# Copies between engines, the rank of the experts and four held-back output pairs in a fused attention and mixture-of-experts kernel

## The chip, the cores and the metric

The kernel runs on one core of one Trainium2 chip. The metric is the device time of one execution in microseconds. Before the change three timed executions took 368.27, 366.48 and 367.61 us; their median is 367.61 us. Inputs and outputs lie in the chip's HBM, and all arithmetic is on the core.

## What is computed

Two blocks follow each other. The first is a linear attention over 8 batches of 576 tokens, 8 heads of 64 values each: the state kv = kᵀv of each head is multiplied by q, normed by its root mean square and scaled by `g_norm`. The second is a mixture of 8 experts over the 4608 tokens of 512 values that come out. A token with a positive score against `w_skip` goes through the one expert that its gate picks.

```
kv  = einsum('bhsd,bhse->bhde', k, v)
o   = einsum('bhsd,bhde->bhse', q, kv)
x   = o / sqrt(mean(o*o, -1) + 1e-6) * g_norm          # as rows: N = 4608, D = 512
out = x.copy()
for the rows with x @ w_skip > 0:
    e      = argmax(x @ w_gate)                         # of 8 experts
    out[row] = x + softmax(x @ w_gate)[e] * (relu(x @ w1[e]) @ w2[e])
```

## The kernel before

All instructions stand in an order that the program itself writes out (`tc.manual_schedule()`), so each engine executes its list strictly in that order, and a waiting instruction holds up all that stands behind it on its engine or queue.

**The attention part** runs over 36 units (`units`): a unit is a half of the heads (u = 0 or 1) for four of the nine token groups of a batch; a pair of units (u = 0 and 1) makes one output tile `xb` of x, 128 x 1024 values, called pair `nq`. Every fourth batch is followed by two units for the ninth token group of the four batches. One step n of the loop over `NU + 2` steps issues, in this order: `turn(n + 1)`, which transposes q of the next unit on TensorE (line 460) and copies it out on ScalarE (L463); `root(n - 1)`, a square root on ScalarE (L529); the jobs of part "early"; `values(n)`, the products q·kv on TensorE (L498, or L508 for the ninth group) and their squares on ScalarE (L514); the jobs of part "mid"; `norm(n - 1)` on VectorE (L536, the reciprocal; L545, `xl` = the product scaled); `squares(n)`, the sums of squares on VectorE (L522); the jobs of part "pe"; then the next jobs of the gating streams. From step 30 on `squares(n)` stands ahead of `norm(n - 1)`. `values` writes one of two PSUM buffers `o_ps`, or `sum_ps` at two steps near the end. GpSimd multiplies `xl` by `g_norm` into `xb` (L615).

**The state of a batch** (`state`, `state_t`, `state_m`) is made in steps ahead of the batch's own units: matmuls k·v (L383) into `sum_ps`, a copy `both` on ScalarE (L390), two transposes (L400) and the logit columns of the state (L408, into the PSUM bank `g_ps`, copied to the `kvd` tiles by ScalarE, L412). Each head pair of `both` also goes to `kvd` in two places: `own` by GpSimd (L395) and `other`, 64 x 256 values that change their partitions, by VectorE (L394, two copies a batch).

**Gating** works in three groups of token tiles (`ends` = 12, 22, 36). For a group, `choose` finds each token's expert on VectorE (ending with `ohb`, L685), `rank` counts on TensorE into the same bank `g_ps` which place a token takes in its expert's list (L696, L699, L702), and `number` turns this into numbers (`pr`, `top`, `s_i`, `lo_i`, `hi_k`, and the one-hot rows `oha_k`, L728). After the second group, when 22 of 36 tiles are known, `rank_experts` sorts the experts by their counts; the order is read back into registers of the DMA queue SyncE (`order_i`, L814), which can then load the first expert's weights w1 (L337). `early` finds the first 192 rows of the first expert: `put` places them on TensorE (L924, 22 matmuls that read `bv`, L904), sums them on VectorE (L928), and gathers their x from the output in HBM by indirect DMAs on GpSimd (L917); TensorE turns these rows (L848, waiting for the gather) and starts the first expert's first layer (L859).

**DMA queues.** SyncE (SP) issues the loads of k, v and q (L118), most stores of x (L653; L642 for the ninth group), and the weights (L337 for w1, L347 for w2). GpSimd issues the first half of every second pair's store (L649) and all indirect DMAs. The stores of two pairs (8 and 9) are held back until step 24 (`store_from`, `starts[B - 3] + 2`). The tile `room`, 128 x 4096 values, is the place of the first expert's w2; until that load it holds small setup data in its first and third quarter. The load of w2 is issued at step 32, behind `values(32)`.

**The expert part** runs on from there over the 8 experts, each with its own w1 and w2 (2 MB each), gathers of its rows, two layers, and scattered stores. The change does not touch it.

Of the kernel before, what the change touches and what calls it, by code (L numbers as in the profile page):

```python
# [8 lines left out]
FP32 = mybir.dt.float32  # L9
BF16 = mybir.dt.bfloat16  # L10
I32 = mybir.dt.int32
# [6 lines left out]
def kernel(  # L18
# [227 lines left out]
    nc.vector.tensor_copy(out=ebase[:, :], in_=ebase_i[:, :])  # L246
    exp_f = keep.tile([P, E], FP32)
# [106 lines left out]
    kvTs, boths = {}, {}  # L354
# [5 lines left out]
    def other(b, w):  # L360

        return kvds[b % KVD][(1 - w) * 64:(2 - w) * 64, w, 1 - w, :, :]
# [12 lines left out]
    def state(b, some):  # L375

        kt, vt = kts[b], vts[b]
        for i in some:
            u, c = divmod(i, C)
            for w in range(2):  # L380
                for a in range(2):
                    r = slice(a * 64, (a + 1) * 64)
                    nc.tensor.matmul(  # L383
                        out=sum_ps[w * 64:(w + 1) * 64, a, u, :],
                        lhsT=kt[r, 2 * u + w, c, :], rhs=vt[r, 2 * u + w, c, :],
                        start=(c == 0), stop=(c == C - 1), skip_group_check=True)
        if some.stop < 2 * C:
            return
        both = att_pool.tile([P, 2, 2 * D], FP32, tag="both", name="both", bufs=1)
        nc.scalar.copy(out=both[:, :, :].rearrange("p u (a d) -> p a u d", a=2), in_=sum_ps)  # L390
        boths[b] = both
        cols = slice(G, G + 2 * D)
        for w in range(2):
            nc.vector.tensor_copy(out=other(b, w)[:, :, cols], in_=both[w * 64:(w + 1) * 64, :, :])  # L394
            nc.gpsimd.tensor_copy(out=own(b, w)[:, :, cols], in_=both[w * 64:(w + 1) * 64, :, :])  # L395

    def state_t(b):
        both = boths.pop(b)
# [223 lines left out]
    store_from = {x[0]: starts[B - 3] + 2 for x in units if x[1:3] in ((0, None), (4, 0))}  # L622
# [12 lines left out]
    def store_x(nq, b, i):  # L635
# [11 lines left out]
        first = int(i == 1 and b < B - 1)  # L647
# [119 lines left out]
    order_i = keep.tile([1, E], I32)  # L767
# [7 lines left out]
    def rank_experts():  # L775

        key = count_tokens("key", gat_pool)
        nc.vector.scalar_tensor_tensor(out=key[:, :], in0=key[:, :], scalar=float(E),
                                       in1=eorder[:, :], op0=ALU.mult, op1=ALU.add)
# [16 lines left out]
        order_f = gat_pool.tile([P, E], FP32, tag="order_f", name="order_f")  # L796
        yield
        nc.vector.tensor_reduce(out=order_f[:, :], in_=gt[:, :, :], axis=AX.X, op=ALU.add)
        yield
        nc.vector.tensor_copy(out=order_i[:, :], in_=order_f[0:1, :])  # L800
# [3 lines left out]
            in0=order_f[:, :].unsqueeze(2).to_broadcast([P, E, CK]), scalar=float(RSPACE // 128),  # L804
# [91 lines left out]
    def early():  # L896
# [24 lines left out]
        def put():  # L921
            scale(now[0])
            for t in range(NE):
# [3 lines left out]
            rows = gat_pool.tile([P, 2], FP32, tag="rows1", name="rows1")  # L927
            nc.vector.tensor_reduce(out=rows[:, :], in_=ps.rearrange("p (c i) -> p c i", i=2),  # L928
                                    axis=AX.X, op=ALU.add)
            gather(rows[:, 0:1], P, 0)  # L930

            def put_more():
# [4 lines left out]
            at(now[0], "pe", put_more)  # L937
# [26 lines left out]
    for b, n in starts.items():  # L964
        if b:
# [8 lines left out]
            at(step, "early", lambda b=b: state_t(b))  # L974
            at(step, "pe", lambda b=b: state_m(b))
# [7 lines left out]
    def gating(g):  # L983

        yield from choose(g)
        yield lambda: rank(g)
# [9 lines left out]
    streams = []  # L996
# [12 lines left out]
    for n in range(NU + 2):  # L1009
        now[0] = n  # L1010
        if 1 <= n < NU - 1:
            turn(n + 1)
# [615 lines left out]
```

## Time and profile before

| | before |
|---|---|
| timed executions | 368.27, 366.48, 367.61 us (median 367.61) |
| the profiled execution | 366.29 us |
| its span, first to last instruction | 364.4 us |
| mean granted TensorE clock | 0.994 |
| busy: TensorE, VectorE, ScalarE, GpSimd | 349.5, 249.2, 145.1, 125.7 us |
| read and written in HBM | 66.80 MB, 14.48 MB |

The profiled execution's own time is 1.9 us longer than its span: that is what lies around the first and the last instruction. The attention part ends near 118 us of the span, the expert part takes the rest. TensorE (PE) is called busy almost throughout, but its matmuls are pipelined and their ends modelled, so what counts is where the profile shows it idle and what ended that idle time. Rows of the timeline give the start, the duration, the engine, the line and the operation, a count if several are merged, and in brackets the idle time of the engine just ahead with what released it. "PEld" is TensorE's weight load, which runs beside its matmuls.

### The profile page before, as it was taken

The numbers are of one execution on the slowest core, as the hardware profiler recorded it, in microseconds if no ns is written. First come the engines' busy times: TensorE is split into PE (matmuls) and PEld (weight loads), VectorE is DVE, ScalarE is ACT, GpSimd is POOL, SyncE is SP. The second block draws the span as 40 slices with busy tenths as digits, with TensorE's granted clock in tenths as the row PEclk, the third lists the DMA queues.
The fourth block names the chain that finished last, engine by engine and source line by source line (L and its number), as shares of the span: only waits on it lengthen the run. The fifth ranks groups of instructions, "written<-read, shape, count | busy, mean of one in ns | idle before, by whom it ended". The sixth has DMA issues, their size and how long they took to land.

```text
span 364.4 us, 9568 instructions
## 1 busy us (share of the span) xinstructions
PE 349.5 (96%) x3754; PEld 305.5 (84%) x3754; DVE 249.2 (68%) x637; ACT 145.1 (40%) x418; POOL 125.7 (34%) x205
## 2 busy tenths in 40 slices
PE   8979998999899999999999999999999999999994
PEld 4769987888779669599879978989988998989983
DVE  2545677889888563876937676786776776878831
ACT  2537775676666244244104402512421530431420
POOL 8036777677776072123041102303203203002003
PEclk9989999999999999999999999999999999999999
DMA  8999999999797369873535537455563762601001
GB/s 272 387 390 377 371 392 398 394 394 384 247 335 255 104 208 379 340 262 89 209 107 205 171 124 254 121 224 176 175 230 98 250 235 53 243 1 58 3 2 54
DMA packets 32808, 81.70 MB, mean 224 GB/s; under 512 B 3242, under 2 KB 3250, under 8 KB 32756
## 3 DMA queue, kind: packets, MB, share of 16 engines
q1 hardware_dynamic: 28944, 69.48, 53.7%
q0 software_dynamic: 3792, 11.53, 9.3%
q8 instruction: 31, 0.51, 0.5%
q14 instruction: 21, 0.17, 0.1%
q10 hardware_dynamic: 20, 0.02, 0.0%
HBM read 66.80 MB, written 14.48 MB: 223 GB/s over the span
## 4 chain that ended last, share of the span: by engine, by line
PE 79%; issue 6%; DMA 5%; DVE 5%; POOL 2%; ACT 2%; SPq 0%; POOLq 0%; DVEq 0%; ACTq 0%
PE bank L1252 46%; PE bank L1184 9%; PE o_ps L498 6%; PE sum_ps L383 4%; PE bank L1172 3%; PE q_ps L460 3%; DMA v<-in_v_dram 2%; PE bank L1153 2%; DVE xl L545 1%; DMA xg<-out_dram,src 1%; PE g_ps L859 1%; DMA xg<-out_dram,asrc 1%; PE q_ps L859 1%; PE o_ps L479 1%; DVE rs L522 1%
## 5 line engine op out<-in xcount | busy, mean ns | idle before, releaser
L1262 ACT COPY p<-bank 128x128 f32<-128x128 f32 (+6 forms) x70 | 20.8, 297 | 96.1 <-PE bank L1252 94.6
L1252 PE MATMUL bank<-xt,w 128*128 128x128 f32 (+5 forms) x336 | 55.4, 288 | 0.1
L1383 POOL DMA_INDIRECT out_dram<-xg,rows x14 | 13.9, 996 | 116.2 <-DVE xg L1380 113.0
L1252 PEld LDWEIGHTS bank<-xt,w 128*128 128x128 f32 x336 | 47.0, 190 | 1.9 <-DVE bank L1256 1.4
L615 POOL TENSOR_TENSOR xb<-xl,g_b 128x512 f32<-128x512 f32 x34 | 41.3, 1216 | 18.1 <-DVE rs L536 16.1
L1256 DVE TENSOR_TENSOR bank<-bank,p 128x128 f32<-128x128 f32 (+6 forms) x70 | 23.6, 337 | 29.7 <-PE bank L1252 28.7
L498 PE MATMUL o_ps<-kvd,qT 128*128 128x146 f32 x240 | 36.0, 293 | 1.3 <-DVE xl L545 1.0
L1252 PE MATMUL bank<-xs,s 128*128 128x128 f32 (+5 forms) x224 | 36.7, 288 | 0.0
L498 PEld LDWEIGHTS o_ps<-kvd,qT 128*128 128x128 f32 x240 | 32.1, 192 | 2.1 <-DVE xl L545 1.8
L1252 PEld LDWEIGHTS bank<-xs,s 128*128 128x128 f32 x224 | 31.1, 190 | 1.0 <-ACT p L1262 0.8
L1184 PE MATMUL bank<-w,ht 128*32 128x128 f32 (+2 forms) x424 | 29.9, 313 | 0.0
L522 DVE TENSOR_REDUCE rs<-sq 128x8 f32<-128x512 f32 x36 | 24.5, 681 | 5.4 <-ACT sq L514 5.2
L545 DVE TENSOR_TENSOR xl<-o_ps,rs 128x584 f32<-128x584 f32 x32 | 24.5, 767 | 4.3 <-DVE rs L536 0.5
L1184 PEld LDWEIGHTS bank<-w,ht 128*32 128x32 f32 (+2 forms) x424 | 18.2, 119 | 10.6 <-issue 7.2
L1252 PE MATMUL bank<-t,ht 128*128 128x256 f32 x112 | 27.0, 384 | 0.0
L1252 PE MATMUL bank<-w,ht 128*128 128x256 f32 x112 | 26.5, 380 | 0.0
L383 PE MATMUL sum_ps<-v,k 64*64 64x64 f32 x1152 | 23.5, 223 | 3.0 <-issue 2.6
L1144 POOL DMA_INDIRECT xg<-out_dram,src x14 | 14.3, 1024 | 34.8 <-DMA out_dram<-xg,rows 18.0
L514 ACT ACTIVATE sq<-o_ps 128x512 f32<-128x512 f32 x34 | 20.3, 596 | 14.1 <-PE o_ps L498 13.2
L383 PEld LDWEIGHTS sum_ps<-v,k 64*64 64x64 f32 x1152 | 19.6, 134 | 7.1 <-issue 3.9
L1252 PE MATMUL bank<-t,hs 128*128 128x256 f32 x112 | 25.3, 379 | 0.0
L1252 PEld LDWEIGHTS bank<-t,ht 128*128 128x128 f32 x112 | 20.8, 190 | 3.9 <-issue 1.2
(216 smaller groups left out, 665.2 us busy)
## 6 DMA issues: line engine op xcount, KB each, us to landing
w<-in_moe_w_dram SPq DMA_DIRECT2D x16, 2048.0 KB, 9.0
k<-in_k_dram SPq DMA_DIRECT2D x32, 288.0 KB, 6.0
v<-in_v_dram SPq DMA_DIRECT2D x32, 288.0 KB, 6.3
q<-in_q_dram SPq DMA_DIRECT2D x32, 288.0 KB, 6.2
out_dram<-xb SPq DMA_DIRECT2D x29, 256.0 KB, 6.1
out_dram<-xb POOLq DMA_DIRECT2D x7, 256.0 KB, 6.4
xg<-out_dram,src POOLq DMA_INDIRECT x16, 3.6
out_dram<-xg,rows POOLq DMA_INDIRECT x16, 6.1
```

The lines of the kernel that those rows point to most:

```text
L383: nc.tensor.matmul(out=sum_ps[w * 64:(w + 1) * 64, a, u, :], lhsT=kt[r, 2 * u + w, c, :], rhs=vt[r, 2 * u + w, c, :], start=(c == 0), stop ...
L498: mm = nc.tensor.matmul(out=ps[:, w, 0:2 * PK].rearrange("p (r k) -> p r k", r=2)[:, :, cols], lhsT=qT[:, w, a, :], rhs=kvds[b % KVD][:, w ...
L514: nc.scalar.activation(out=sq[:, :, :, :], in_=heads(ps, G, G + 2 * D), func=ACT.Square)
L522: nc.vector.tensor_reduce(out=rs[:, :, :], in_=sq[:, :, :, :].rearrange("p x y (a d) -> p x (y a) d", a=2), axis=AX.X, op=ALU.add)
L545: nc.vector.tensor_tensor(out=xl[:, :, :, :].rearrange("p x y (a k) -> p x (y a) k", a=2), in0=ps[:, :, 0:2 * PK].rearrange("p x (h k) -> ...
L615: late.append((lambda eng: eng.tensor_tensor(out=xb[:, :, 4 * u * D:(4 * u + 4) * D].rearrange("p r (w x) -> p r w x", w=2), in0=xl[:, :, ...
L1144: nc.gpsimd.indirect_dma_start(out=x_of(xg, off, m), out_offset=None, in_=cut_rows(m)[:, :], in_offset=bass.IndirectOffsetOnAxis(ap=idx[:, ...
L1184: nc.tensor.matmul(out=yps[q * m:(q + 1) * m, 0:n], lhsT=ht(f)[:, off:off + m], rhs=w_sb[r][1][:, f, q * n:(q + 1) * n], start=(f == 0), s ...
L1252: nc.tensor.matmul(out=out, lhsT=lhsT(i), rhs=rhs(i), start=start and i == 0, stop=i == k - 1, skip_group_check=True)
L1256: nc.vector.tensor_tensor(out=to, in0=x, in1=y, op=ALU.add)
L1262: nc.scalar.copy(out=t, in_=x)
L1383: ins = nc.gpsimd.indirect_dma_start(out=cut_rows(m)[:, :], out_offset=bass.IndirectOffsetOnAxis(ap=rows[:, col:col + 1], axis=0), in_=x, ...
```

## The change

The change has five parts.

1. **Held-back pairs.** The x of pairs 2 to 5 (both halves of batches 1 and 2) is written into the four quarters of `room` in place of `xb` buffers, and all eight half stores of 256 KB go out on SP behind the last load of q at step 24, in place of six on SP and two on GpSimd at various steps ahead.
2. **Copies across.** For batches 5, 6 and 7 (`ACROSS` = 5) the two `other` copies go from VectorE to ScalarE: one behind `kvT`, one behind the squares of the same step.
3. **Ranks ahead.** `rank` of the first two groups goes from part "pe" to part "mid", so that TensorE does it directly behind `values`, ahead of `state_m`.
4. **Fewer sums for the order of the experts.** The counts come in one step with a constant `kbase` = `eorder` - 8 `ebase`, and the reduction writes `order_i` as integers at once; one subtraction and one cast fall away.
5. **Sums beside the placing.** `put` turns q of step 32 at once behind the 22 placing matmuls; the sum of the rows, both gathers and the small matmul `more` stand behind `squares(30)`. Two empty turns of the stream keep `put` at step 30, so that `lo_i`, `oha_k` and `bv` come a step earlier than they did relative to it.

```diff
@@ state
         for w in range(2):
-            nc.vector.tensor_copy(out=other(b, w)[:, :, cols], in_=both[w * 64:(w + 1) * 64, :, :])
+            if b < ACROSS:
+                nc.vector.tensor_copy(out=other(b, w)[:, :, cols], in_=both[w * 64:(w + 1) * 64, :, :])
             nc.gpsimd.tensor_copy(out=own(b, w)[:, :, cols], in_=both[w * 64:(w + 1) * 64, :, :])
+    def state_across(b, w):
+        if b >= ACROSS:
+            nc.scalar.copy(out=other(b, w)[:, :, G:G + 2 * D], in_=boths[b][w * 64:(w + 1) * 64, :, :])
@@ weigh
-            xbs[nq] = xb_pool.tile([P, 2, DM], FP32, tag="xb", name="xb")
+            if nq in IN_ROOM:
+                x = room[:, IN_ROOM.index(nq) * 2 * DM:(IN_ROOM.index(nq) + 1) * 2 * DM]
+                xbs[nq] = x.rearrange("p (r d) -> p r d", r=2)
+            else:
+                xbs[nq] = xb_pool.tile([P, 2, DM], FP32, tag="xb", name="xb")
...
-    store_from = {x[0]: starts[B - 3] + 2 for x in units if x[1:3] in ((0, None), (4, 0))}
+    IN_ROOM = range(2, 6)
+    store_from = {nq: starts[B - 3] + 2 for nq in (*IN_ROOM, 4 * NQ, 4 * NQ + 1)}
@@ store_x
-        first = int(i == 1 and b < B - 1)
+        first = int(i == 1 and b < B - 1 and nq not in store_from)
@@ rank_experts
-        key = count_tokens("key", gat_pool)
-        nc.vector.scalar_tensor_tensor(out=key[:, :], in0=key[:, :], scalar=float(E),
-                                       in1=eorder[:, :], op0=ALU.mult, op1=ALU.add)
+        key = gat_pool.tile([P, E], FP32, tag="key", name="key")
+        nc.vector.scalar_tensor_tensor(out=key[:, :], in0=top[:, :], scalar=float(E),
+                                       in1=kbase[:, :], op0=ALU.mult, op1=ALU.add)
...
-        nc.vector.tensor_reduce(out=order_f[:, :], in_=gt[:, :, :], axis=AX.X, op=ALU.add)
-        yield
-        nc.vector.tensor_copy(out=order_i[:, :], in_=order_f[0:1, :])
+            nc.vector.tensor_reduce(out=order_i[:, :], in_=gt[:, :, :], axis=AX.X, op=ALU.add)
@@ early: put
-            rows = gat_pool.tile([P, 2], FP32, tag="rows1", name="rows1")
-            nc.vector.tensor_reduce(out=rows[:, :], in_=ps.rearrange("p (c i) -> p c i", i=2),
-                                    axis=AX.X, op=ALU.add)
-            gather(rows[:, 0:1], P, 0)
-
-            def put_more():
+            turn(now[0] + 2)
+            turned_ahead.append(now[0] + 2)
+
+            def put_rows():
+                rows = gat_pool.tile([P, 2], FP32, tag="rows1", name="rows1")
+                nc.vector.tensor_reduce(out=rows[:, :], in_=ps.rearrange("p (c i) -> p c i", i=2),
+                                        axis=AX.X, op=ALU.add)
+                gather(rows[:, 0:1], P, 0)
...
-            at(now[0], "pe", put_more)
+            at(now[0], "squared", put_rows)
+        yield
+        yield
         yield "mid", put
@@ the states' steps
             at(step, "early", lambda b=b: state_t(b))
+            for w, part in enumerate(("early", "mid")):
+                at(step, part, lambda b=b, w=w: state_across(b, w))
@@ gating
-        yield lambda: rank(g)
+        yield "mid", lambda: rank(g)
@@ the loop over the steps
-        if 1 <= n < NU - 1:
+        if 1 <= n < NU - 1 and n + 1 not in turned_ahead:
             turn(n + 1)
...
             squares(n)
+        jobs(n, "squared")
```

Three places show how the change moves instructions. A row is a line of the program, the operation, and output<-input with the shape; "x4" merges four alike.

TensorE, step 24, before. `q_ps` is the transposed q of step 25, `o_ps` the products of step 24, `sum_ps` a part of the state of batch 7, and `g_ps` takes in turn the transposed state, its logit columns and the rank of the second group:

```order
L460 MATMUL q_ps<-ident,q 128x2x64 x4
L400 MATMUL g_ps<-ident,both 128x128 x2
L498 MATMUL o_ps<-kvd_161,qT 128x2x73 x4
L408 MATMUL g_ps<-gw_b,kvT 128x36 x2
L383 MATMUL sum_ps<-v,k 64x64 x16
L696 MATMUL g_ps<-top,ident 128x88
L699 LDWEIGHTS ut
L699 MATMUL g_ps<-ohb,ut 128x80
```

The same place in the changed kernel, where L709, L712 and L715 are the rank and L416 the logit columns; first the head of the rank, then its end:

```order
L468 MATMUL q_ps<-ident,q 128x2x64 x4
L408 MATMUL g_ps<-ident,both 128x128 x2
L506 MATMUL o_ps<-kvd_161,qT 128x2x73 x4
L709 MATMUL g_ps<-top,ident 128x88
L712 LDWEIGHTS ut
L712 MATMUL g_ps<-ohb,ut 128x80
```

```order
L715 LDWEIGHTS ones
L715 MATMUL g_ps<-ohb,ones 128x8
L416 MATMUL g_ps<-gw_b,kvT 128x36 x2
L386 MATMUL sum_ps<-v,k 64x64 x16
L468 MATMUL q_ps<-ident,q 128x2x64 x4
```

The rank now stands ahead of the logit columns, and so also ahead of ScalarE's copies that read them. The first group's rank, at step 16, moves in the same way.

VectorE, from the end of step 27 to step 29, before. `rs` is the sum of squares and its reciprocal, `xl` the normed product, `kvd<-both` the copies across of batch 7, and the rest the gating of the second group:

```order
L394 COPY kvd_167<-both 64x2x128 x2
L721 TENSOR_SCALAR lo_i<-s_i 128x10
L723 TENSOR_SCALAR hi_k<-s_i 128x10
L728 TENSOR_TENSOR oha_k<-row_i,lo_i 128x256 x2
L536 RECIPROCAL rs<-rs 128x8
L545 TENSOR_TENSOR xl<-o_ps,rs 128x584
L522 TENSOR_REDUCE rs<-sq 128x8
L728 TENSOR_TENSOR oha_k<-row_i,lo_i 128x256 x3
L899 TENSOR_TENSOR ohc_1975<-hi_k,colid_i 128x44
```

And in the changed kernel:

```order
L736 TENSOR_SCALAR hi_k<-s_i 128x10
L741 TENSOR_TENSOR oha_k<-row_i,lo_i 128x256 x3
L544 RECIPROCAL rs<-rs 128x8
L553 TENSOR_TENSOR xl<-o_ps,rs 128x584
L530 TENSOR_REDUCE rs<-sq 128x8
L741 TENSOR_TENSOR oha_k<-row_i,lo_i 128x256 x2
L910 TENSOR_TENSOR ohc_1970<-hi_k,colid_i 128x44
L915 TENSOR_TENSOR bv_1972<-ohc_1970,row_k 128x88
```

The two copies are gone, `lo_i` stands a step earlier, and `bv`, which the placing reads, moved up by one reciprocal, `xl` and `rs`.

VectorE behind that, before: the placed rows' sum and the first gather's indices stand ahead of the `rs` of step 30, the second gather's behind the norm.

```order
L904 TENSOR_TENSOR bv_2002<-ohc_1975,row_k 128x88
L928 TENSOR_REDUCE rows_2044<-g_ps 128x2
L913 TENSOR_SCALAR row_2047<-rows_2044,q_f_237 128x1
L915 SCALAR_TENSOR_TENSOR src_2046<-row_2047 128x1
L522 TENSOR_REDUCE rs<-sq 128x8
L536 RECIPROCAL rs<-rs 128x8
L545 TENSOR_TENSOR xl<-o_ps,rs 128x584
```

And in the changed kernel:

```order
L530 TENSOR_REDUCE rs<-sq 128x8 x2
L943 TENSOR_REDUCE rows_2048<-g_ps 128x2
L924 TENSOR_SCALAR row_2051<-rows_2048,q_f_239 128x1
L926 SCALAR_TENSOR_TENSOR src_2050<-row_2051 128x1
L924 TENSOR_SCALAR row_2057<-g_ps,q_f_250 128x1
L926 SCALAR_TENSOR_TENSOR src_2056<-row_2057 128x1
```

The sum of the rows and the first gather's indices moved behind the `rs` of step 30, and the second gather's came up to them.

More of the change, by code (lines that the diff above doesn't have):

```diff
@@ L766 @@
     colid_i = keep.tile([P, NCOL], I32)
-    order_i = keep.tile([1, E], I32)
+    order_i = keep.tile([P, E], I32)
     is_at = keep.tile([P, E, E], FP32)
@@ L994, in gating @@
             yield from early()
-    streams = []
+    streams, turned_ahead = [], []
     now = [0]
```

12 lines of the change are left out of this document (8 added, 4 removed).

## The prediction

> **What bounds the kernel now.** I looked first at the page's chain of work that ended last (PE 79% of it), then at the table of busy time by stretches, to see where TensorE is not full, and then at the timeline there. TensorE is full but for its first 30 us and a few places between 60 and 105 us, all in the part that the change touches.
>
> ```profile
> core 0: us, PE busy (x) PEld busy (x) DVE busy (x) ACT busy (x) POOL busy (x), PEclk, DMA share, GB/s
> 60.00:65.00 5.00, 4.04 (x126) 3.50 (x115) 3.13 (x10) 2.69 (x9) 2.64 (x7) 1.00 1.05 396
> 80.00:85.00 5.00, 4.34 (x103) 3.86 (x104) 4.63 (x12) 3.61 (x11) 3.96 (x7) 1.00 1.03 373
> 90.00:95.00 5.00, 5.00 (x76) 4.53 (x74) 4.57 (x14) 3.56 (x11) 3.90 (x9) 1.00 0.54 169
> 95.00:100.00 5.00, 3.33 (x34) 2.98 (x33) 4.43 (x12) 3.00 (x10) 3.95 (x7) 1.00 0.98 352
> ```
>
> TensorE lacks 0.96 us in the first of these stretches, 0.66 in the second and 1.67 in the last; in the third it lacks nothing. The DMA engines are saturated up to 85 us, but TensorE does not wait for them there.
>
> The chain of waits in order of time shows what bounds the last stretch: VectorE, up to a gather that TensorE then waits for.
>
> ```profile
> 93.04 0.29 DVE kvd L394
> ...
> 93.76 0.27 DVE lo_i L721
> 94.10 1.02 DVE oha_k L728 x2
> 95.37 0.77 DVE xl L545
> 96.72 1.09 DVE oha_k L728 x3
> ...
> 98.95 0.59 DVE rs L522
> 99.54 0.17 DVE bv L904
> ...
> 100.48 0.17 DVE rows L928
> ...
> 101.37 5.18 DMA xg<-out_dram,src
> 106.69 0.63 PE q_ps L848 x4
> 108.43 0.89 PE g_ps L859 x8
> ```
>
> From L848 on, TensorE has its work in a row up to the expert part, whose loads follow TensorE's own progress. So whatever L848 gains or loses goes to the end. The question is only how much earlier L848 starts.
>
> **The ranks.** The timeline at the first group's rank:
>
> ```profile
> 60.23 0.27 DVE L685 TENSOR_TENSOR ohb<-eorder,fi 128x96 bf16<-128x96 f32 x1
> 60.46 0.64 PE L408 MATMUL g_ps<-gw_b,kvT 128*128 128x36 f32 x4
> 62.05 0.47 PE L696 MATMUL g_ps<-top,ident 128*128 128x104 f32 x2 [0.96 <-ACT kvd L412]
> ```
>
> The rank stands behind the logit columns and waits until ScalarE has read them out of the same bank. In the new order it follows `values`, and what it needs, `ohb`, is ready at 60.50, when `values` ends (L408 starts at 60.46). Nothing reads the bank then but the copy `kvT`, which L408 needs too. The wait of 0.96 us goes. The logit columns come later by the rank's length, under 1 us, and ScalarE's four copies with them; they are for units a step away. Next is the transposed q of unit 18, then `qT`, the root and `xl`, which move up by almost as much (ScalarE ends its copies some 0.65 us later, just as q is there). I take **-0.9**, bounded by 0 and -1.07 (the weight load's idle time).
>
> The second group's rank, at step 24:
>
> ```profile
> 81.80 1.16 PE L498 MATMUL o_ps<-kvd,qT 128*128 128x146 f32 x8
> 82.01 0.73 DVE L394 COPY kvd<-both 64x256 f32<-64x256 f32 x2
> 83.13 0.49 DVE L685 TENSOR_TENSOR ohb<-eorder,fi 128x80 bf16<-128x80 f32 x1
> 84.40 0.46 PE L696 MATMUL g_ps<-top,ident 128*128 128x88 f32 x2 [0.45 <-ACT kvd L412]
> ```
>
> The idle 0.45 us goes in the same way if `ohb` is there when `values` ends, at 82.96. Before, it ends at 83.62. But the two copies ahead of it (0.73 and the gap) leave VectorE, so it ends at 82.86. The parts hang together: without the copies' move the rank would wait 0.66 us for `ohb`. I take **-0.45**; between 0 (`ohb` late again) and -0.66 (all that the stretch lacks).
>
> **The transfers held back.** Eight half stores, 2 MB, leave the queue ahead of the loads of q and k, v. TensorE has no wait for them now, so this is worth nothing by itself, but it carries the gain above: the q of unit 18 is issued here,
>
> ```profile
> 53.84 3.43 SPq L118 DMA_DIRECT2D q<-in_q_dram  x4
> DMA to landing us min/median/max: 3.2/6.2/7.5
> ```
>
> so its first two parts land at about 60 to 61.5, and TensorE now wants them at 61.9 instead of 62.8. Two stores of 256 KB less ahead at 390 GB/s are 1.3 us. Without this cover up to half of the -0.9 would be in doubt. At the other end, SP now has this in front of the first expert's weights:
>
> ```profile
> 78.02 6.06 SPq L118 DMA_DIRECT2D q<-in_q_dram  x8
> 85.77 2.85 SPq L653 DMA_DIRECT2D out_dram<-xb  x3
> 92.71 0.42 SPq L337 DMA_DIRECT2D w<-in_moe_w_dram  x1
> ```
>
> The loads of q for batch 6 come some 5 us earlier, those of batch 7 can't (their buffer is free only when step 24 has turned q, L460 ahead of 81.8), then come eight stores, the five old ones, and the experts' order. The bytes up to w1 are the same as before, so I leave w1 at about 92.7. Its cover: stores issued behind it
>
> ```profile
> L653 SPq DMA_DIRECT2D out_dram<-xb x2: 553/568/582, 93.8 to 94.5; - x2
> DMA to landing us min/median/max: 9.4/9.4/9.4
> ```
>
> landed by 103.2 to 103.9, while L859, its first use, comes at 108.4. Some 4.5 to 5 us are left. I take **0**, and price the loss of this cover below.
>
> **The chain to the gather.** Up to the `rs` of step 29, VectorE loses the copies (93.04 to 93.76, 0.72 us) and `lo_i` (0.34 with its gap, moved to where TensorE has more work than VectorE); one `oha_k` (0.36, a third of 1.09) moves a step up, and `bv` takes its place behind `ohc`. At the `xl` of 95.37 that is 0.72 + 0.34 - 0.36 = 0.70 us, and at the `rs` of 98.95 it is 0.70 + 0.36 - 0.21 = 0.85. Since ScalarE's root must fit in between, I use 0.73. Then the new order takes it back: before, from the end of `rs` (99.54) to `rows` (100.48) it is 0.94 us by `bv` and the 22 matmuls. Now it is the root, the squares, and the `rs` of step 30:
>
> ```profile
> 99.57 0.30 ACT L529 ACTIVATE rs<-rs,eps_t 128x8 f32<-128x8 f32 x1 [0.95 <-DVE rs L522]
> 99.78 0.58 ACT L514 ACTIVATE sq<-sum_ps 128x512 f32<-128x512 f32 x1
> 101.00 0.68 DVE L522 TENSOR_REDUCE rs<-sq 128x8 f32<-128x512 f32 x1
> ```
>
> 99.54 to 100.36 are 0.82, 0.68 for the sum and two gaps of 0.03 make 1.56: 0.62 more. The gather comes 0.73 - 0.62 = **0.1** earlier. Bounds: +0.6 (no VectorE time arrives) and -0.85 (the squares are done sooner). The small matmul `more` now makes TensorE wait for `rows`, with the products of step 31 behind it; but the products of step 32 waited for `xl` of step 29 anyway, so I cost it at nothing; uncovered it is about 1 us.
>
> The gather took 5.18 us. Other gathers of the kernel:
>
> ```profile
> L1144 POOL DMA_INDIRECT xg<-out_dram,src x14: 953/978/1464, 129.7 to 288.8; - x14
> DMA to landing us min/median/max: 2.9/3.6/7.1
> ```
>
> Since it now starts 1.4 us nearer to w1, it can as well take longer; between 3.6 and 7.1, and I keep 5.2 as the row that is the same place: **0**, from -1.6 to +1.9. [...]
>
> **ScalarE's copies.** A copy of that size on ScalarE:
>
> ```profile
> L482 ACT COPY q<-o_ps x15: 353/356/373, 16.5 to 103.5; 64x256 f32<-64x256 f32 x15
> ```
>
> Six of them are 2.1 us, two to a step; the first fits into ScalarE's idle time ahead of the squares (it waits for TensorE there), the second delays the four small copies by 0.36. I take **0**, up to +0.35 in each of the last two such steps. [...]
>
> The two instructions saved for the experts' order (some 0.35 us) and the setup of `kbase` lie where TensorE is full: 0.
>
> **Sum.** -0.9 - 0.45 - 0.1 = **-1.45 us**. From the profiled execution's 366.3 (its span of 364.4 and 1.9 around it) that is 364.8. That execution is the fastest of the four shown, 1.3 under the median of 367.6; against their mean, 367.2, it makes 365.7, and I say **365.8**.
>
> **The rivals.**
>
> *The gather eats the gain.* VectorE gets to the rows no earlier, or the gather takes 5.8 to 6.2 because w1 and the eight stores are still moving. For it: L848 waited for the gather before already, and everything ahead of it then only makes this wait longer. Against it: the gather starts earlier by all that TensorE gains. The kernel gains 0 to 0.9: 366.3 to 367.2.
>
> *More than the sum.* The DMA engines are emptier at 100 us, since w1 lands ahead of the gather, and it takes 3.6 to 4.5: 0.7 to 1.6 more, a gain of 2.1 to 3.1, 364.1 to 365.1. For it: the loads of q are no longer behind 2 MB of stores. Against it: these stores are now nearer to the gather.
>
> *Slower: w1 comes late.* SP stands at batch 7's q until TensorE has turned step 24's q, with nothing in front; the DMA engines run empty, and then 2 MB at 390 GB/s are 5.4 us more between q and w1. If 3 us of emptiness come on top, w1 is 8.4 us later. From 5 us on each one counts in full: L859 starts 3.4 us later, and the kernel takes 369.7 on the profile's scale. For it: a queue in order, and the reading of the experts' order (88.6 to 92.7) hidden by nothing. Against it: the same bytes went in front of w1 before, and an emptied queue lets SP issue faster.
>
> **How the numbers follow.** The forecast has 0.45, the gather 0.18, more than the sum 0.25, slower 0.12. The range reaches from the second rival's gain to the first steps of the third: 363.9 to 368.4. A measurement of this kernel tells about 0.5%, 1.8 us, from no change. The second rival and a small part of the forecast are faster by more than that, 0.32; the slower one, 0.12; the rest, 0.56, is within.
>
> **What would show it.** In the profile after, no idle time ahead of either rank; no L394 after 70 us, and `xl` of step 27 some 0.7 us nearer to the `rs` ahead; the gather starting about 100.0 and L848 at 105.3. The forecast is wrong if TensorE waits for a load of q or for `ohb`, if w1 is issued after 97, or if the gather takes other than 4.6 to 5.8.

## The result and the profile after

The changed kernel took 371.88 us (median of six runs, 370.96 to 374.46), the kernel before 367.17 us (six runs, 366.10 to 368.27). The ratio is **1.0141**, with a 95% interval of 1.0115 to 1.0167: slower by some 5 us, outside the range that was predicted. The profiled execution took 374.46 us with a span of 372.7; it is the slowest of the six. Below, a time is the median of all executions of a kernel; a ratio is taken to executions of the kernel before beside them, and leaves out single executions that took over 1.5% more than the fastest of their kernel.

Where the change acts as forecast, the profile after shows it. TensorE does both ranks without idle time ahead of them, no copy across is left on VectorE after 70 us, and the wait ahead of the products of step 29 fell from 1.02 us to 0.38. The timeline of TensorE after, the two ranks and that step:

```profile
60.07 0.47 PE L709 MATMUL g_ps<-top,ident 128*128 128x104 f32 x2
...
64.49 0.57 PE L386 MATMUL sum_ps<-v,k 64*64 64x64 f32 x21 [1.75 <-issue]
...
84.05 0.35 PE L709 MATMUL g_ps<-top,ident 128*128 128x88 f32 x2
...
96.73 1.26 PE L506 MATMUL o_ps<-kvd,qT 128*128 128x146 f32 x8 [0.38 <-DVE xl L553]
```

The row of step 29 in the timeline of the kernel before:

```profile
96.19 1.26 PE L498 MATMUL o_ps<-kvd,qT 128*128 128x146 f32 x8 [1.02 <-DVE xl L545]
```

But behind the first rank, at 64.49, stands a wait of 1.75 us for "issue" (time in which the engine waited for nothing that the profile shows), which the profile of the kernel before does not have there. It comes back below.

The large loss is further on. SP's timeline after, from the loads of q for batches 6 and 7 to the first expert's weights:

```profile
73.97 10.38 SPq L118 DMA_DIRECT2D q<-in_q_dram  x8
84.39 7.82 SPq L666 DMA_DIRECT2D out_dram<-w  x8
92.31 2.35 SPq L655 DMA_DIRECT2D out_dram<-xb  x2
94.75 3.06 SPq L666 DMA_DIRECT2D out_dram<-xb  x3
102.06 0.42 SPq L340 DMA_DIRECT2D w<-in_moe_w_dram  x1
```

The eight loads of q, the first ones issued early and the last ones held until their buffer is free, keep SP for 10.38 us where it was 6.06 before. Only then come the eight held stores (`w` is the name of the room's tile), and w1 goes out at 102.06 in place of 92.71. The table by stretches shows what the DMA engines (the last two columns, share and GB/s) did meanwhile, and the clock ahead of them:

```profile
core 0: us, PE busy (x) PEld busy (x) DVE busy (x) ACT busy (x) POOL busy (x), PEclk, DMA share, GB/s
80.00:82.00 2.00, 2.00 (x52) 1.78 (x50) 1.32 (x7) 1.43 (x4) 0.64 (x3) 1.00 0.10 38
82.00:84.00 2.00, 1.79 (x14) 1.55 (x15) 1.85 (x6) 1.95 (x6) 1.71 (x3) 1.00 0.21 33
100.00:102.00 2.00, 1.08 (x24) 0.85 (x22) 1.11 (x4) 1.72 (x5) 1.32 (x2) 1.00 0.16 53
112.00:120.00 8.00, 7.99 (x59) 7.40 (x58) 4.51 (x17) 3.22 (x12) 1.88 (x4) 0.50 1.03 390
```

From 80 to 84 the engines are nearly empty (share 0.10 and 0.21): SP stands at a load that can't start (its longest wait for TensorE's `q_ps`, L468, is 5.6 us), and 2 MB that could go stand behind it. Before, the stretch from 80 to 85 moved 373 GB/s. TensorE's timeline then shows what waits:

```profile
109.65 0.63 PE L859 MATMUL q_ps<-ident,xg 128*128 128x128 f32 x4 [2.42 <-DMA xg<-out_dram,src]
...
111.56 0.66 PE L859 MATMUL q_ps<-ident,xg 128*128 128x128 f32 x2 [0.61 <-DMA xg<-out_dram,src]
112.23 2.07 PE L870 MATMUL g_ps<-xt_first,w 128*128 128x128 f32 x8
...
115.42 4.63 PE L870 MATMUL g_ps<-xt_first,w 128*128 128x64 f32 x16
```

The same two rows of the first layer (L859 then) in the timeline of the kernel before:

```profile
108.27 1.06 PE L859 MATMUL g_ps<-xt_first,w 128*128 128x128 f32 x8
...
109.92 2.46 PE L859 MATMUL g_ps<-xt_first,w 128*128 128x64 f32 x16
```

The gather was issued at 102.54, with w1 half a microsecond ahead of it, and its rows landed 7.0 us later. The weights held the first layer up for less, as the row of its weight load in the kernel after shows:

```profile
112.23 1.78 PEld L870 LDWEIGHTS g_ps<-xt_first,w 128*128 128x128 f32 x8 [0.41 <-DMA w<-in_moe_w_dram]
```

Then the same products took almost twice as long, 4.63 against 2.46 us: the granted clock is 0.50 from 111.2 to 121.4.

Counted up between the two profiled executions: the products of step 33 start at 105.97 against 105.23 (+0.7), the first layer at 112.23 against 108.27 (+4.0), and the last matmul at 366.65 against 358.66 (+8.0). So 3.2 us arise where TensorE waits for the gather (3.0 us) and its weight load for w1 (0.4), and the other 4 us behind that, for the most part at half clock. In the six runs the mean clock lay between 0.983 and 0.992 (mean 0.9865); in 27 runs of the kernel before, taken later beside the first experiments, its mean is 0.9948. By this, 0.0083 of some 370 us, an estimate of 3.1 us of the loss is clock.

### The profile page after: what moved, and what is told of

It is laid out like the page before. It is cut to its first block, busy times and chain, and to the rows that moved or that the text cites. A ratio compares the mean times of both kernels' runs of the same rounds, so it can differ in the third digit from the quotient of the medians.

```text
span 372.7 us, 9558 instructions
## 1 busy us (share of the span) xinstructions
PE 354.1 (95%) x3754; PEld 308.8 (83%) x3754; DVE 246.6 (66%) x630; ACT 147.9 (40%) x424; POOL 125.8 (34%) x203
## 4 chain that ended last, share of the span: by engine, by line
PE 80%; issue 7%; DMA 5%; DVE 3%; POOL 2%; ACT 2%; SPq 0%; POOLq 0%; DVEq 0%; ACTq 0%
PE bank L1271 45%; PE bank L1203 9%; PE o_ps L506 6%; PE sum_ps L386 5%; PE bank L1191 4%; PE q_ps L468 3%; DMA v<-in_v_dram 3%; PE bank L1172 2%; DMA xg<-out_dram,src 2%; PE g_ps L870 2%; DVE xl L553 1%; PE q_ps L870 1%; PE g_ps L416 1%; PE o_ps L487 1%; PE g_ps L408 1%
## 5 line engine op out<-in xcount | busy, mean ns | idle before, releaser
L1275 DVE TENSOR_TENSOR bank<-bank,p 128x128 f32<-128x128 f32 (+6 forms) x70 | 23.6, 337 | 29.7 <-PE bank L1271 28.9
L627 POOL TENSOR_TENSOR xb<-xl,g_b 128x512 f32<-128x512 f32 x26 | 31.8, 1221 | 18.6 <-DVE rs L544 12.9
L386 PE MATMUL sum_ps<-v,k 64*64 64x64 f32 x1152 | 25.0, 223 | 5.9 <-issue 4.6
L386 PEld LDWEIGHTS sum_ps<-v,k 64*64 64x64 f32 x1152 | 20.5, 134 | 10.6 <-issue 7.4
L1163 POOL DMA_INDIRECT xg<-out_dram,src x14 | 15.1, 1080 | 34.5 <-DMA out_dram<-xg,rows 11.6
L522 ACT ACTIVATE sq<-o_ps 128x512 f32<-128x512 f32 x34 | 20.3, 596 | 13.9 <-PE o_ps L506 10.2
```

What stands on the lines that cost most here:

```text
L386: nc.tensor.matmul(out=sum_ps[w * 64:(w + 1) * 64, a, u, :], lhsT=kt[r, 2 * u + w, c, :], rhs=vt[r, 2 * u + w, c, :], start=(c == 0), stop ...
L522: nc.scalar.activation(out=sq[:, :, :, :], in_=heads(ps, G, G + 2 * D), func=ACT.Square)
L627: late.append((lambda eng: eng.tensor_tensor(out=xb[:, :, 4 * u * D:(4 * u + 4) * D].rearrange("p r (w x) -> p r w x", w=2), in0=xl[:, :, ...
L1163: nc.gpsimd.indirect_dma_start(out=x_of(xg, off, m), out_offset=None, in_=cut_rows(m)[:, :], in_offset=bass.IndirectOffsetOnAxis(ap=idx[:, ...
L1275: nc.vector.tensor_tensor(out=to, in0=x, in1=y, op=ALU.add)
```

## The experiments

Theory 1: all of the loss comes from part 1, the held-back stores. The rivals put it on the rows' sum behind the squares (A) or on the copies and ranks (B).

**Part 1 taken back.**

```diff
-    IN_ROOM = range(2, 6)
+    IN_ROOM = range(0)
```

> The changed kernel with part 1 alone taken back: no pair in the w2 room, all stores at the steps of before. Theory 1 (the eight stores behind the last q load push w1 back, and that costs the whole loss): w1 is issued near 92.5 us again in place of 102.06, the gather lands in about 5.2 us in place of 7.2 to 7.5, no half clock after 110 us, and the time is 365.0 to 366.7, below the kernel before by what the prediction summed (about 1.4). Rival A (the loss comes from the rows' sum behind the squares, which starts the gather later): w1 is early, yet the gather still starts near 102.5, and the time stays above 369. Rival B (the copies on ScalarE or the ranks ahead slow the steps from 40 to 80 us): TensorE's idle time there stays as in the changed kernel, and the time is 368 to 370.

Measured: 367.86 us (12 runs), ratio 0.9995 (0.9975 to 1.0016). The loss is gone, and so are the late w1 and the wait for the gather, as SP's and TensorE's timelines show:

```profile
94.44 0.42 SPq L340 DMA_DIRECT2D w<-in_moe_w_dram  x1
```

```profile
65.36 0.57 PE L386 MATMUL sum_ps<-v,k 64*64 64x64 f32 x21 [2.00 <-issue]
...
108.98 0.60 PE L859 MATMUL q_ps<-ident,xg 128*128 128x128 f32 x4
```

Rivals A and B fall. But the time is not below the kernel before either, where theory 1 had 365.0 to 366.7: what parts 2 to 5 were to bring isn't seen.

**Part 1 alone on the kernel before** (its lines of `weigh`, `store_from` and `first`, nothing else).

> The kernel before with part 1 alone: four pairs in the room, eight stores behind the last q load. Theory 1: w1 is issued at 101 to 103 us, the first layer of the first expert waits for it or for the gather beside it, and the time is 370.5 to 373. Rival A or B (the loss is in the other parts): 367 to 368, as before.

Measured: 372.61 us, ratio 1.0126 (1.0091 to 1.0160). w1 went out at 101.74, and of TensorE's waits one line carries it:

```profile
PE q_ps L853 <- DMA xg<-out_dram,src: 3.0, 1, 3.0
```

(in total, times, longest). Taking part 1 away and putting it in alone give the same answer: theory 1 holds.

**The held stores between the two loads of q.**

```diff
-    store_from = {nq: starts[B - 3] + 2 for nq in (*IN_ROOM, 4 * NQ, 4 * NQ + 1)}
+    store_from = {**{nq: starts[B - 3] + 1 for nq in IN_ROOM},
+                  **{nq: starts[B - 3] + 2 for nq in (4 * NQ, 4 * NQ + 1)}}
```

> The changed kernel with the eight held stores one step earlier, so that they stand on SP between the q loads of batch 6 and batch 7, in the time in which SP waits for the buffer of batch 7's q. Theory 1 (what costs is that the DMA engines run empty while SP waits, and 2 MB come after): the stores fill that gap, w1 is issued at 93 to 97 us and the time is 365 to 367.5. Rival C (holding the stores costs by itself, by the bytes in front of w1 wherever they stand): w1 stays later than 99, and the time is 369 to 372. A late q of batch 7 would show as idle time of TensorE ahead of L468 at step 26 to 28.

Measured: 370.33 us, ratio 1.0046 (1.0016 to 1.0076). SP's timeline:

```profile
74.60 3.27 SPq L118 DMA_DIRECT2D q<-in_q_dram  x4
77.92 7.14 SPq L666 DMA_DIRECT2D out_dram<-w  x8
85.16 3.86 SPq L118 DMA_DIRECT2D q<-in_q_dram  x4
...
96.96 0.42 SPq L340 DMA_DIRECT2D w<-in_moe_w_dram  x1
```

The stores now fill the gap (DMA share 0.97 and 0.99 from 80 to 84 us, where it was 0.10 and 0.21). From the start of step 24's products to the issue of w1 it is 11.4 us here, 10.9 before, 10.3 without held stores, but 19.0 in the changed kernel and 18.7 with part 1 alone. So the place is what made w1 late, not the bytes. The time is another matter: theory 1 had 365 to 367.5, and 370.33 lies in rival C's range. The clock is lower again, 0.9887 in the mean of 12 runs against 0.9948, and 0.0061 of 370 us is 2.3 us, an estimate as large as the loss that is left (1.7 us by the ratio). The one profile has its half clock in two stretches, and neither is at the gather (behind the busy times a row has clock, DMA share and GB/s; a clock of 0.83 over 10 us is 3.4 us at half):

```profile
20.00:30.00 10.00, 7.85 (x155) 7.38 (x147) 3.19 (x7) 3.39 (x9) 4.03 (x8) 0.83 1.04 376
60.00:70.00 10.00, 7.79 (x171) 6.90 (x163) 6.34 (x18) 4.63 (x14) 6.12 (x12) 0.83 1.05 383
110.00:120.00 10.00, 8.54 (x117) 8.05 (x118) 7.57 (x23) 6.43 (x24) 6.25 (x13) 1.00 0.89 317
```

In each of the first two TensorE waited for "issue" (2.15 us up to 25.38, 1.72 us up to 66.44), in the third 1.70 us for the gather. Whether this order makes such stretches more frequent, and so whether the stores cost something there too, stayed open.

**Idle time of TensorE filled**, to see if it brings the half clock.

```diff
+    at(NU - 3, "pe", lambda: dense(9, ps_q.tile([P, 512], FP32, tag="q", name="q_ps")))
     for part in range(2):
         at(NU - 3 + part, "pe", lambda part=part: first_in(part))
```

> The changed kernel with nine more idle-filling products of ones (about 2.4 us by the three at 105 us, which took 0.81) ahead of the first turned rows of the gather, where TensorE had 2.42 us of idle time; their result is read by nobody. Theory 2 (the half clock from 111.4 to 121.3 us is the answer to that idle time and to the thin work around it): the clock stays at 1.0, the wait is covered, and the time is 367 to 369, some 3 to 5 below the changed kernel. Rival D (the half clock has another cause, or comes anyway): half clock again after 110 us, and 371 to 373.

Measured: 371.56 us, ratio 1.0094 (1.0066 to 1.0123). Of the ten executions the profiled one is by far the slowest (374.94 us); the median of the other nine, 370.75 us, lies between the two forecasts. The profile has no half clock between 90 and 150 us, though the gather took 8.1 us and TensorE still waited for it:

```profile
PE q_ps L859 <- DMA xg<-out_dram,src: 1.6, 1, 1.6
```

It has half clock elsewhere, from 24.7 and from 65.7 us, beside waits for "issue" of 2.43 and 2.27 us. The mean clock of the runs rose from 0.9865 to 0.993. So the runs speak for the idle time as what brings the half clock at that place. By the two ratios some 1.7 of the 5 us came back, less than the 3.1 us estimated from the clock; the two intervals just overlap.

### Why parts 2 to 5 gained nothing

TensorE's weight loads and matmuls, numbered in the order of their starts, show that the waits for "issue" stand at fixed numbers (worked out from the records; us of each wait over 0.3):

```
number              688    1440   2198   2451   3211
before              2.60   -      -      -      -
before, again       2.42   -      0.84   0.74   -
part 1 alone        2.29   0.69   0.32   0.84   -
changed             1.60   0.65   1.75   0.57   -
without part 1      2.42   0.65   2.00   0.74   1.02
first rank back     2.70   0.36   1.13   -      -
```

They are about 252 apart or a multiple of that, and each ends 1.3 to 1.5 us after a packet of 16 KB on the queue that the profile calls "instruction". The view of the DMA queues for 61 to 64 us of the changed kernel has one (packets, MB, share), beside the queue of the loads:

```profile
q1 hardware_dynamic: 559, 1.15, 103.2%
q8 instruction: 1, 0.02, 2.3%
```

Theory 3: TensorE's next 16 KB of program come over the same DMA engines as the loads, which are full there (103.2% for the loads' queue alone), and a stretch of 253 instructions can't be shorter than that takes. (That these packets are what TensorE waits for, and that the full engines are what makes them slow, is argued, not shown: the engines' share is about 1.0 at all of these waits, so there is nothing to compare with.) The stretch from the 1945th to the 2198th holds the first group's rank. Without the waits at its end it took 5.70 us before, with the rank's wait of 0.96 in it, and 4.61 in the changed kernel; with them 5.70 (6.82 in the second profile) and 6.57.

**The first rank alone back, the kernel before once more, and both kernels with 48 instructions more ahead.** The edits on the changed kernel without part 1; the second also on the kernel before:

```diff
-        yield "mid", lambda: rank(g)
+        yield "mid" if g else "pe", lambda: rank(g)
```

```diff
-    dense(11)
+    dense(6)
+    for _ in range(29):
+        nc.tensor.matmul(out=warm_ps[:, 0:P], lhsT=ones[:, :], rhs=ones[:, :], start=True, stop=True)
```

> The changed kernel without part 1, and with the rank of the first group (only that) back in part pe, behind the logit columns. Theory 3 (the 0.96 us that the rank ahead frees are given back at the 2198th instruction, where the program isn't there yet): the wait for ScalarE of about 1 us is back, the stall behind it shrinks to 0 to 0.5 us, and the time is the same or up to 1 us lower than without it, 366.9 to 367.9. The prediction's sum (the rank ahead is worth 0.9 by itself): 368.5 to 369.

> The kernel before, for a second profile of it. If the stalls of theory 3 vary from execution to execution: again one of 2 to 2.6 us at the 688th instruction, and at the 1440th, 2198th and 2451st anything from 0 to 1 us. If the kernel before has only the one at the 688th, the three others stay at 0.

> The kernel before with 48 more instructions on TensorE at its head: of the eleven warm-up products of ones 128 x 512 five go, and 29 of 128 x 128 come, in about the same time. Nothing else moves. Theory 3 (TensorE stalls at fixed numbers of instructions, at the 688th, 1440th, 2198th, 2451st and 3211th, because its next 16 KB of program come over the same DMA engines as the loads; a stretch of some 253 instructions can't be shorter than the about 6.1 us that this takes): the stalls keep their numbers and so fall on products that stand 48 places earlier in the program; in these stretches there is then more of the longer work, and worked out from the stretches of the profile before the stalls shrink from 4.8 to 2.3 us. The time is 365.0 to 366.5, some 1.5 to 3 below the kernel before. Rival E (the stalls belong to the products or their data, k and v): they stay with the same products, 48 numbers later, and the time is as before, 367 to 368.5.

> The changed kernel without part 1 (all stores at the steps of before), with the same 48 instructions at TensorE's head. Theory 3: its stalls, 6.8 us in its profile without the 48, shrink to about 3, and the time is 364 to 365.5; beside the kernel before with the same shift it gains some 1 us, a part of the 1.45 that parts 2 to 5 were to bring. Rival E: the stalls stay, and the time is 367 to 368.5. Rival F (parts 2 to 5 bring nothing in any case): the same time as the kernel before with the shift, within 0.3.

Measured: with the first rank back 366.89 us, 0.9996 (0.9979 to 1.0012), the same as with the rank ahead (0.9995). Its timeline has the rank's wait again, and a shorter one behind it than the 2.00 us without part 1, though not the 0 to 0.5 us that was expected:

```profile
62.60 0.47 PE L709 MATMUL g_ps<-top,ident 128*128 128x104 f32 x2 [0.96 <-ACT kvd L420]
...
65.95 0.57 PE L386 MATMUL sum_ps<-v,k 64*64 64x64 f32 x21 [1.13 <-issue]
```

So the first rank ahead is worth nothing that is seen, not 0.9; the two intervals together leave about 1 us open. The second profile of the kernel before (367.48 us in its one run) has waits of 0.84 and 0.74 us at the 2198th and the 2451st, where the first one has none: the first one was lucky there.

The shifted kernels took 367.16 us (1.0010, 0.9987 to 1.0033) and 367.57 us (1.0015, 0.9996 to 1.0034): no gain in either, where theory 3 had one for both; the times lie in rival E's ranges. The waits did stay with their numbers, as theory 3 has it: at the 688th, 1.22 us in the one and 0.50 in the other, and none at the 736th, where rival E would have them. (At the 1191st both have 0.8 and 0.7 us, which the profile puts down to a copy of ScalarE; an "instruction" packet ends 1.5 us ahead of the first and 2.1 us ahead of the second, so they tell less.) The shifted kernel without part 1 was 1.7 us ahead of the kernel before at step 16 and 2.0 at step 20. Then it lost this, and the table of TensorE's waits says to what:

```profile
PE q_ps L470 <- DMA q<-in_q_dram: 2.6, 4, 1.1
```

It had run into the loads of q, on DMA engines that are full from 10 to 90 us (the table by stretches of the same kernel, share 1.04; the kernel before has 1.04 too):

```profile
10.00:90.00 80.00, 74.70 (x1518) 64.38 (x1514) 55.28 (x156) 51.74 (x137) 48.88 (x93) 1.00 1.04 383
```

The start of the products of a step, less that of the first profile of the kernel before (us, from the records):

```
step                 16     18     20     24     25     28     29     31     33
before, again       +0.1   +0.8   +1.8   +1.7   +1.7   +1.7   +1.7   +1.7   +1.7
without part 1      -0.4   +0.9   +2.0   +2.3   +1.8   +3.1   +2.5   +2.7   +2.7
first rank back     +0.5   +1.5   +2.0   +2.4   +1.8   +1.9   +1.2   +1.4   +1.4
without 1, shifted  -1.7   -2.1   -2.0   -0.4   +0.4   +0.5   -0.1   +0.1   +0.1
changed             -0.4   +0.1   +0.9   +1.3   +0.7   +1.2   +0.5   +0.7   +0.7
```

The gain of the second rank (step 24 to 25, -0.5) is in every row of the changed kernel that did not wait for a load there, that of the copies and `lo_i` taken off VectorE (step 28 to 29, -0.6) in all. But at step 33 these four rows spread over 0.1 to 2.7 us, and the two executions of one kernel, the one before, are 1.7 us apart: gains of half a microsecond can't be told from that.

**Fewer bytes ahead of these loads**: pairs 2 and 3 alone held, their four stores on ScalarE's queue, behind the loads of q; with the shift, on both kernels, and then in two milder forms. The edit, cut, against the shifted kernel without part 1:

```diff
+    HELD = starts[B - 2]
-    IN_ROOM = range(0)
+    IN_ROOM = range(2, 4)
-    store_from = {nq: starts[B - 3] + 2 for nq in (*IN_ROOM, 4 * NQ, 4 * NQ + 1)}
+    store_from = {**{nq: HELD for nq in IN_ROOM}, 4 * NQ: starts[B - 3] + 2, 4 * NQ + 1: starts[B - 3] + 2}
...
             for hf in range(first, 2):
-                nc.sync.dma_start(out=rows[hf], in_=x[hf * 64:(hf + 1) * 64, :])
+                eng = nc.scalar if nq in IN_ROOM else nc.sync
+                eng.dma_start(out=rows[hf], in_=x[hf * 64:(hf + 1) * 64, :])
```

> The changed kernel with the 48 instructions at TensorE's head, and of part 1 only pairs 2 and 3 in the room (1 MB of stores); these four half stores go out on ScalarE's queue at the end of step 26, in place of SP's. Theory 4 (in the shifted kernel without held stores TensorE waits 2.6 us for loads of q, since it runs ahead of DMA engines that are full from 10 to 90 us; the DMA engines are empty for about 2 us while SP reads the experts' order, near 91 to 94): 1 MB less ahead of these loads takes 1.5 to 2.6 us of these waits away, w1 stays within 1 us of 92.9, and the time is 365.0 to 366.3. Rival G (the held bytes come out of the gather's or w1's time wherever they go): w1 lands late or the gather takes over 6 us, and the time is 367 or more.

> The kernel before with the same 48 instructions and the same two pairs held for ScalarE's queue, without parts 2 to 5. Theory 4: it had no wait for a load of q in its shifted profile, so that there is little to gain: 366.3 to 367.2. The changed kernel's parts 2 to 5 are then worth the difference between this kernel and the one above, by the prediction's sum 1.45 less what the stretches of the program still take (0.5 to 1.0). If both come out the same within 0.3 us, parts 2 to 5 bring nothing even where neither the program nor the loads hold TensorE up.

Measured: 370.30 us, 1.0024 (0.9996 to 1.0053), and 371.07 us, 1.0052 (1.0030 to 1.0075), where the kernel before took 369.38 us beside them. The difference between the two, 0.8 us with an uncertainty of some 1.3, leaves both nothing and the 1.45 of the prediction possible for parts 2 to 5. The waits for q are gone (theory 4, as far as it goes), and both were 0.9 and 1.3 us ahead of the first profile at step 27. Then ScalarE stood in the four issues, the last three of which took 3.65 us in the first of the two,

```profile
88.22 0.54 ACTq L670 DMA_DIRECT2D out_dram<-w  x1
88.80 3.65 ACTq L670 DMA_DIRECT2D out_dram<-w  x3
```

and TensorE waited 1.7 and 2.2 us for `qT`, which it copies. w1 went out at 95.3 and 95.7. Neither forecast had ScalarE's part. The last two kernels issue the stores one a step, of two pairs (steps 24 to 27) and of pair 2 alone (steps 25 and 26):

> The same as the shifted kernel with pairs 2 and 3 held, but the four half stores go out one at the end of each of the steps 24 to 27, in place of four together, which held ScalarE for 4.2 us and TensorE for 2.6. Theory 4: the lead of 0.9 us over the kernel before that the kernel with four together had at step 27 stays to the end, ScalarE loses 0.5 us at a time, w1 goes out by 94.5, and the ratio to the kernel before is 0.995 to 0.999. Rival G (the held 1 MB comes out of w1's and the gather's time): TensorE waits for the gather, and the ratio is 1.000 to 1.004.

> The same with pair 2 alone held (two half stores, 512 KB, at the end of steps 25 and 26). Theory 4: half of the waits for loads of q stay (1.3 of 2.6 us), w1 goes out at 93 to 93.5, the ratio is 0.996 to 1.000. Rival G: between the one above and 1.0015, the ratio with no store held.

Measured: 370.21 us, 1.0062 (1.0033 to 1.0091), and 368.80 us, 1.0042 (1.0017 to 1.0067), both above theory 4's ranges. With two pairs w1 is late again (99.42), the gather keeps TensorE waiting for 3.0 us, and ScalarE stands for 2.1 us ahead of the fourth store, so that TensorE waits 2.2 us for it; rival G had 1.000 to 1.004. With one pair the ratio is in rival G's range, w1 goes out at 92.80, and TensorE waits 1.5 us for the gather. But this profile is of the fastest of twelve executions (365.41 us; they reach to 371.12), and in it the gather landed 0.3 us earlier than in the kernel before. What makes the other executions slow was not seen. So that the held bytes come out of w1's or the gather's time is likely, not shown. No version beat the kernel before.

**The gather and w1 in all profiles.** The records of twelve profiles (two have no landing time) show what a gather takes by how far w1 went out ahead of it (us):

```
                       w1 ahead by   gather took   landed after w1 went out
changed                    0.5           7.0           7.5
part 1 alone               0.9           8.0           8.9
idle time filled           0.9           8.1           8.9
two pairs, one a step      2.9           7.6          10.4
pair 2, one a step         7.3           6.1          13.4
held between               8.1           6.3          14.4
before                     8.7           5.2          13.8
before, shifted            8.8           5.1          14.0
without 1, shifted         9.0           5.3          14.3
first rank back            9.3           4.8          14.0
before, again              9.5           4.3          13.8
without part 1            10.0           3.9          13.9
```

Where w1 went out 7 us or more ahead, the gather landed 13.4 to 14.4 us after w1, whenever it was issued itself. In the kernel before TensorE waits only 0.2 us for it. By this pattern, bringing the gather's issue forward without w1's would bring little, as the prediction's first rival has it. It is a pattern over single executions with other transfers in flight; no run isolates it.

## Why the prediction was wrong, point by point

- **The transfers held back: the step that failed.** It said: "The bytes up to w1 are the same as before, so I leave w1 at about 92.7". The bytes are the same, but SP's queue, in order, did not move them while it stood for 5.6 us at a load that couldn't start; w1 went out at 102.06, 19.0 us after the start of step 24's products in place of 10.9. The same bytes one step earlier in the queue put it back to 11.4. The third rival had this mechanism, down to "the DMA engines run empty" and an issue 8.4 us later (measured 9.35). It got a chance of 0.12 because equal bytes were weighed against it, and a faster issue into an emptied queue (the four loads of q at 82.59 did take 1.75 us, where four at 53.84 took 3.43 before; but the eight stores behind them took 7.82), though the text itself knew that batch 7's q couldn't start before step 24 had turned its own. When SP could go on was to be counted, not what it carries. Two signs that the prediction itself named for being wrong came true: w1 after 97, and a gather outside 4.6 to 5.8 us.
- **Its price was too low**: 369.7 on the profile's scale, where the profiled execution took 374.46 (the slowest of six; 3.4 us above the median of before would be 370.6, against a median of 371.88). Missing were the gather beside w1 (7.0 us for 5.18; the bound of +1.9 was there, but for another case) and the half clock after the wait, which no term had. The sum had 0 for a gather nearer to w1: it took 1.8 to 2.9 us more than the 5.18 of before where w1 went out less than 1 us ahead.
- **The cover of w1**, 4.5 to 5 us, came out near, in part by luck: w1 went out 9.35 us later, and TensorE's first product with it came 3.96 us later. But 0.7 of this was there at step 33 already, and what TensorE mostly waited for was the gather beside w1 (3.0 us), for w1 itself 0.4.
- **The first rank, -0.9: worth nothing that is seen.** The wait went, as said. But when asked what is late next, the step named q, `qT` and `xl`; next was a wait of 1.75 us for "issue", by theory 3 for TensorE's own program. The profile before showed such a wait at 23.86 (2.6 us), which the prediction left out as lying in "its first 30 us".
- **The second rank, -0.45: right** (-0.5 from step 24 to 25).
- **The chain to the gather, -0.1: right.** From the products of step 28 to the gather it is 8.23 us before and 8.22 without part 1. The wait of TensorE for `rows` (0.92 us) is there, and the steps behind it start no later for it.
- **ScalarE's copies, 0 to 0.35: near.** They hold `xl` up at step 22; from step 21 to 22 it is 0.3 us more with them. Each took 0.41 us, not 0.36.
- **TensorE does not wait for the DMA engines** up to 85 us: true for that profile; that TensorE was just late enough for it is the author's reading. In the shifted kernel without part 1, which was up to 2.1 us earlier there, it waited 2.6 us for them.
- **A slip in the range:** its lower end, 363.9, is said to be the second rival's gain, which is 364.1. Nothing hangs on it.

## What to carry to other kernels

Before moving transfers to a later place in an in-order queue, look what they will stand behind: here SP stood for 5.6 us at a load that waited for its buffer, with 2 MB behind it; the DMA share fell to 0.10 and 0.21 from 80 to 84 us, and w1 went out 9.35 us later. Where the engines are full for a long stretch (share 1.04 from 10 to 90 us), count a wait taken off TensorE ahead of it as a gain only as far as what it waits for next is there earlier too: the shifted kernel without part 1, 2.0 us ahead at step 20, then waited 2.6 us for loads of q, and behind the rank that lost its wait of 0.96 us stood 1.75 and 2.00 us of "issue" (changed, and without part 1). One profile shows one execution: waits for "issue" differed between two profiles of one kernel by 1.4 us, as much as the change was to bring.

## What the runs showed of the hardware

- **TensorE waits at fixed numbers of its instructions.** The waits for "issue" in the table above took up to 2.7 us at a time and in the unshifted kernels 2.6 to 6.8 us in sum, each with a packet of 16 KB on the "instruction" queue 1.3 to 1.5 us ahead of its end. That TensorE waits there for its own program is theory 3's reading: the first wait stayed at the 688th with 48 instructions more ahead (1.22 and 0.50 us), but no run shows its cause.
- **Half clock after short waits.** A clock of 0.50 lasted 3.4 us (the kernel before, from 25.5 to 28.9), 6.8 us (the changed kernel, shifted, with pairs 2 and 3 held, from 94.1) or 10.2 us (the changed kernel, from 111.2), and came after waits of 1.5 to 3.0 us, though not after each (2.42 us in the changed kernel without part 1 brought none). In the kernel before, 2.60 us of idle time, up to 23.86, stood ahead of it.
- **A gather beside w1 is slow.** Issued within 1 us of the 2 MB of w1 it took 7.0, 8.0 and 8.1 us to land; with w1 8 to 9 us ahead 5.1 to 6.3, and with 10 us ahead 3.9.
- **Four stores in a row on ScalarE's queue** held that engine for 4.2 us (shifted kernel, pairs 2 and 3 held); issued by themselves, one took 0.5.
